# Attention maxima by pairs of 64-row matmuls into double banks, one accumulator bank, weighted values in threes, first pair head by head

## The chip, the cores and the metric

The kernel is one program on one core of a Trainium2 chip. Its metric is device time in microseconds (us) of one execution, from a single launch. PE is the matmul engine (PEld its weight loads), DVE the vector engine, ACT the scalar engine, POOL the general engine, SP the engine that issues most DMAs. PE writes its results to PSUM, which has eight banks of 512 fp32 columns on 128 partitions; DVE and ACT read them from there.

## What is computed

Attention over 8 batches of 8 heads, where two neighbouring queries are averaged first, and then a mixture of 8 experts on its output, each expert taking at most 576 tokens in the order of the gate's logits. Only the attention part is touched.

```python
q_pool = q.reshape(B, H, S // factor, factor, D).mean(axis=3)      # 8, 8, 576, 64
scores = scale * np.matmul(q_pool, k.transpose(0, 1, 3, 2))        # 576 x 1152 a head
scores = scores - np.max(scores, axis=-1, keepdims=True)
attn = np.exp(scores)
attn = attn / (np.sum(attn, axis=-1, keepdims=True) + 1e-09)
return np.matmul(attn, v).astype(np.float32)
...
logits = x @ w_gate
...
h = np.maximum(x[mask] @ w1[e], 0.0)
out[mask] = h @ w2[e]
```

## The kernel before

The 64 heads go in 32 pairs; the two heads of a pair lie one below the other on 128 partitions (64 dimensions each). A pair n has these stages.

- **Load and split** (`load`, `split`): queries `QD` and keys `KD` come in by DMA; DVE sums the query halves to `QS`; ACT rounds them to fp32r, `QH` and `KH`; the remainders become `QL` and `KL`. `spread` copies these by DMA into `KA`, `KB`, `QA`, `QB`, one head per slot, high and low parts stacked on 128 partitions.
- **Maxima** (`max_chunk`, line 401): for each block j of 64 queries of both heads a block-diagonal weight `BD[:, j]` (128 x 128) is multiplied with 384 keys of `KH`: 9 blocks times 3 chunks, 27 matmuls of 128 rows. They rotate through the PSUM banks `ma`, `mb`, `mc`, and DVE reduces each to a column of `MX` (line 405). For the first pair five more banks are used, and a third of the maxima goes to `MS` by ACT and is folded there (lines 408, 415, 417).
- **Shift** (`max_end`, `aug`): DVE takes the last maximum into `CM`, PE transposes it (line 437), DVE writes the shift `AU`, and two DMAs put it into row 64 of `QB`. The first pair does it without the DMA, with nine rows and the mask `ndiag` (line 432).
- **Scores** (`step`): 18 steps a pair, head s and key block kb of 128 keys. In each step, two halves of 288 queries: one matmul with `KA`, `QA` (line 466, 128 rows) and one with `KB`, `QB` (line 467, 65 rows) into one of three banks `sc`; ACT takes the exponential to `P` (line 470); POOL, for some steps DVE, computes the remainder `PM` (line 473).
- **Weighted values** (line 483): for every step, 5 query blocks times 3 f16 matmuls of 65 or 64 columns, accumulated over the head's 9 steps in the bank `av[s]`. They are issued for two steps at a time: 30 matmuls in a row. When a head is done, `evac` reads the bank on DVE (lines 506, 507, 510).
- **Gate** (every second pair): PE transposes the result (line 524), ACT copies it, three matmuls with 8 columns each go into strips of `av[1]` (line 536), DVE adds them to `LS`.

The order of the instructions on each engine is made by a planner, `Order`, from costs, priorities (`LEAD`) and due times (`LATE`) when the program is built; every engine then works through its own list in that order. Pair n+1's loads, splits and maxima are spread between pair n's steps. The experts (from line 670) follow with their own planner.

Of the kernel before, what the change touches and what calls it, by code (L numbers as in the profile page):

```python
# [46 lines left out]
class Order:  # L47
# [25 lines left out]
    def emit(self):  # L73
# [85 lines left out]
      0.5093}  # L159
LEAD = {"aug": 5.86, "augd": 4.23, "augt": -25.48, "av0a": 4.05, "bd": 8.85, "expa": -39.43, "expb": 17.79,  # L160
# [4 lines left out]
LATE = {"aug": 100, "augd": -300, "augt": 350, "av0a": 100, "bd": 1400, "expa": 50, "expb": -100, "fill": 3150,  # L165
# [69 lines left out]
def attention(ctx, tc, top, kt, qt, v, wg, x_dram, L, npair=NPAIR):  # L235
# [28 lines left out]
    BD = several(2, [128, NB, 128], FR, "BD")  # L264
# [21 lines left out]
    XT = several(3, [128, 3, 128], F32, "XT")  # L286
# [6 lines left out]
    ndiag = const.tile([128, NB, 64], F32, name="ndiag")  # L293
    iq = scratch[:, 1220:1220 + NB * 64].rearrange("p (a b) -> p a b", b=64)

    def fill(i, t):
        od.add(t, "POOL", 1000, lambda: nc.gpsimd.memset(BD[i].bitcast(F32), 0.0), w=[("BD", i, 0), ("BD", i, 1)], tag="fill")
        od.add(t + .1, "POOL", 100, lambda: nc.gpsimd.memset(CM[i], 0.0), w=[("CM", i, b) for b in range(3)], tag="fill")
        od.add(t + .2, "POOL", 1960, lambda: nc.gpsimd.memset(KB[i].bitcast(F32)[64:64 + NB], 1.0), w=[("KB1", i)], tag="fill")
        od.add(t + .3, "POOL", 90, lambda: nc.gpsimd.memset(V16[i][:, :, :, 128:129], 1.0),  # L300
               w=[("VH", i, 0), ("VH", i, 1)], tag="fill")
        if i == 0:
            od.add(t + .15, "POOL", 1060, lambda: nc.gpsimd.iota(iq, pattern=[[1, NB], [0, 64]], base=64, channel_multiplier=-1),
                   w=["iq"], tag="fill")
            od.add(t + .4, "DVE", 370, lambda: nc.vector.tensor_scalar(ndiag, iq, 0.0, -1.0, op0=OP.is_equal, op1=OP.mult),
                   r=["iq"], w=["ndiag"], tag="fill")
# [21 lines left out]
    def split(n, t):  # L328
# [41 lines left out]
    def values(n, t):  # L370
# [14 lines left out]
        od.add(t + AT["vs"] - 1, "DVE", 442, scale, r=["mb"], w=[("VS", i)], tag="vs")  # L385
# [9 lines left out]
    def max_chunk(n, j, c, z, t):  # L395
        i = n % 2
        banks = [(ma, "ma"), (mb, "mb"), (mc, "mc")]
        if n == 0:
            banks += [(sc[a], ("sc", a)) for a in range(3)] + [(av[b], f"av{b}") for b in range(2)]
        m, mk = banks[z % len(banks)]  # L400
        od.add(t, "PE", 175, lambda: nc.tensor.matmul(  # L401
            m[:, :384], BD[i][:, j, :], KH[i][:, 384 * c:384 * c + 384], start=True, stop=True),
            r=[("BD", i, 0), ("BD", i, 1)] + [("KH", i, z) for z in ((0,), (0, 1), (1,))[c]], w=[mk], tag="mm")
        if n or c < 2:
            od.add(t, "DVE", 464, lambda: nc.vector.tensor_reduce(MX[i][:, j, c:c + 1], m[:, :384], axis=AX.X, op=OP.max),  # L405
                   r=[mk], w=[("MX", i, j, c)], tag="mr")
        else:
            od.add(t, "ACT", 371, lambda: nc.scalar.copy(MS[:, j], m[:, :384]), r=[mk], w=[("MS", j)], tag="mc")

    def fold(j, t):  # L410

        m = MS[:, 3 * j:3 * j + 3]
        keys = [("MS", 3 * j + x) for x in range(3)]
        for z, w in enumerate((192, 96)):
            od.add(t + .01 * z, "DVE", 72 + .54 * w * 3, lambda w=w: nc.vector.tensor_tensor(
                m[:, :, :w], m[:, :, :w], m[:, :, w:2 * w], op=OP.max), r=keys, w=keys, tag="fold", lock=1)
        od.add(t + .05, "DVE", 70 + 300, lambda: nc.vector.tensor_reduce(
            MX[0][:, 3 * j:3 * j + 3, 2], m[:, :, :96], axis=AX.X, op=OP.max), r=keys, w=[("MX", 0, 3 * j + x, 2) for x in range(3)], tag="fold")

    def max_end(n, t):  # L420
        i = n % 2
        od.add(t, "DVE", 92, lambda: nc.vector.tensor_reduce(CM[i][:, 64:64 + NB], MX[i], axis=AX.X, op=OP.max),
               r=[("MX", i, j, c) for j in range(NB) for c in range(3)], w=[("CM", i, 2)], tag="fold")

    def aug(n, t):
        i = n % 2
        r = slice(64, 64 + NB)
        cm = [("CM", i, b) for b in range(3)]
        if n == 0:
            od.add(t, "PE", 110, lambda: nc.tensor.transpose(mb[:64 + NB, :128], CM[i][:, :64 + NB], ident), r=cm, w=["mb"], tag="augt")  # L430
            for s in range(2):
                od.add(t, "DVE", 670, lambda s=s: nc.vector.scalar_tensor_tensor(
                    QB[i][r, s].rearrange("p (a b) -> p a b", b=64),
                    mb[r, None, 64 * s:64 * s + 64].to_broadcast([NB, NB, 64]), -SHIFT, ndiag[r],
                    op0=OP.add, op1=OP.mult), r=["mb", "ndiag"], w=[("QB1", i, s)], tag="aug")
        else:
            od.add(t, "PE", 50, lambda: nc.tensor.transpose(mb[:NB, :128], CM[i][:, 64:64 + NB], ident), r=cm, w=["mb"], tag="augt")
            od.add(t, "DVE", 187, lambda: nc.vector.tensor_scalar(AU, mb[:NB, :128], -SHIFT, -1.0, op0=OP.add, op1=OP.mult),
                   r=["mb"], w=["AU"], tag="aug")
            for s in range(2):  # L440
                od.add(t, "SP", 830, lambda s=s: nc.sync.dma_start(
                    QB[i].bitcast(F32)[64:65, s].rearrange("p (a b) -> p a b", b=64), AU.bitcast(F32)[:, 64 * s:64 * s + 64]),
                    r=["AU"], w=[("QB1", i, s)], late=2000, tag="augd")
# [5 lines left out]
    def step(g):  # L449
# [10 lines left out]
        qr = [(x, i, s) for x in ("KA0", "KA1", "KB", "QA0", "QA1", "QB0", "QB1")] + [("KB1", i)]  # L460
# [15 lines left out]
        o, low, high = av[s], V16[i][:, s, kb, 0:D], V16[i][:, s, kb, D:2 * D + 1]  # L476
# [11 lines left out]
        behind.append((weighted, r, f"av{s}", kb == NKB - 1 and (n, s)))  # L488
        if g % 2:
            two = list(behind)  # L490
            behind.clear()
            od.cur = None
            od.add(g + LAG, "PE", 2 * 5 * 93, lambda: [x[0](range(5)) for x in two], r=two[0][1] + two[1][1],
                   w=[x[2] for x in two][:2 if s == 1 and kb == 0 else 1], tag="av0a", kind=1)
            for x in two:
                if x[3]:
                    evac(*x[3], g + LAG + 0.02)

    def evac(n, s, t):

        r, x = RS[s], X[n // 2 % NX][:, :, n % 2 * D:n % 2 * D + D]
        o = av[s][:, :325].rearrange("p (j d) -> p j d", d=65)
# [10 lines left out]
        od.add(t, "DVE", 346, recip, r=[f"av{s}", ("VS", n % 2)], w=[("RS", s)], tag="rc")  # L513
# [765 lines left out]
```

## Time and profile before

| | |
|---|---|
| median of 3 runs | 1342.98 us (1340.21 to 1343.5) |
| the profiled execution, its own time | 1342.09 us |
| its span, first to last instruction | 1340.3 us |
| PE busy | 97% of the span |
| DVE, ACT, POOL busy | 79%, 59%, 58% |
| attention with all 32 pairs under way | about 40 to 830 us of the span |

A row of a timeline has the start (us from the span's start), the duration, the engine, the line of the kernel, the operation, what it writes and reads, its shapes and how many like it follow each other. For a matmul 64\*128 means 64 rows of weights and 128 columns of them. Ends of matmuls are modelled: the next one starts long before, so their cost is read from one start to the next. In the grouped view, the two numbers behind the bar are busy us and mean ns of one.

### The profile page before, as it was taken

Reading aid. Unit: us, or ns where it says so; the run is one execution under the profiler, and the core shown is the slowest. Engines: PE = TensorE matmul, PEld = TensorE weight load, DVE = VectorE, ACT = ScalarE, POOL = GpSimd, SP = SyncE. Lnnn points to the kernel's source line nnn. Section 1 sums busy time; section 2 is a strip of 40 time slices with the busy share of each in tenths; the row PEclk is TensorE's granted clock in tenths of the full one; section 3 lists DMA queues with packets and bytes.
Section 4 is the critical chain, followed back from the end, with each engine's and each line's share of the span. In section 5 each row is a group of like instructions: output and inputs, shape, how many; then the busy total and the mean of one; then the engine's idle time right before and its main releaser. Section 6 shows DMA issues by size and latency. Waiting matters only on the chain.

```text
span 1340.3 us, 39670 instructions
## 1 busy us (share of the span) xinstructions
PE 1296.5 (97%) x15415; PEld 1169.3 (87%) x15415; DVE 1060.4 (79%) x2901; ACT 788.9 (59%) x1838; POOL 775.6 (58%) x739
## 2 busy tenths in 40 slices
PE   7999999999999999999999999699999999999996
PEld 6889999999999999999999898487979788798895
DVE  8999999999899999999999883788977767662220
ACT  4777777777777777777787765042343334244330
POOL 4555565665565665655655655064777676587631
PEclk8999999999999999999999999899999999999999
DMA  7877877877877877877877750044435343363400
GB/s 213 222 183 195 203 183 185 208 185 177 211 185 177 210 190 177 205 194 177 201 198 175 180 117 20 1 162 169 161 96 185 116 149 122 119 197 124 143 13 35
DMA packets 86841, 213.25 MB, mean 159 GB/s; under 512 B 12796, under 2 KB 37372, under 8 KB 84476
## 3 DMA queue, kind: packets, MB, share of 16 engines
q1 hardware_dynamic: 78172, 158.26, 47.9%
q0 software_dynamic: 8336, 52.44, 11.0%
q8 instruction: 121, 1.98, 0.6%
q14 instruction: 68, 0.56, 0.1%
q10 hardware_dynamic: 144, 0.02, 0.0%
HBM read 99.63 MB, written 18.87 MB: 88 GB/s over the span
## 4 chain that ended last, share of the span: by engine, by line
PE 86%; DVE 6%; DMA 3%; issue 2%; ACT 1%; POOL 0%; SPq 0%; POOLq 0%; DVEq 0%; ACTq 0%
PE av L483 18%; PE ph L1172 16%; PE po L1202 14%; PE sc L466 12%; PE sc L467 10%; PE mb L401 4%; PE mc L401 4%; PE ma L401 3%; DVE MX L405 2%; DMA KD<-in_kt_dram 2%; PE rt L845 1%; PE av L524 1%; PE po L1199 1%; PE av L536 1%; DMA KA<-KH 1%
## 5 line engine op out<-in xcount | busy, mean ns | idle before, releaser
L473 POOL TENSOR_TENSOR PM<-P 128x576 f16<-128x576 f32 x413 | 471.6, 1158 | 345.2 <-ACT P L470 328.1
L470 ACT ACTIVATE P<-sc 128x288 f32<-128x288 f32 x1152 | 433.9, 410 | 161.4 <-PE sc L467 128.1
L466 PE MATMUL sc<-QA,KA 128*128 128x288 f32 x1152 | 361.8, 321 | 2.3 <-ACT P L470 2.1
L467 PE MATMUL sc<-QB,KB 65*128 65x288 f32 (+1 forms) x1152 | 336.4, 298 | 3.1 <-issue 1.7
L483 PE MATMUL av<-V,P 128*128 128x65 f16 (+1 forms) x5760 | 304.0, 193 | 0.0
L483 PEld LDWEIGHTS <-P 128*128 128x128 bf16 x5760 | 270.3, 98 | 26.4 <-issue 2.2
L483 PE MATMUL av<-V,PM 128*128 128x65 f16 x2880 | 291.7, 194 | 0.5 <-DVE PM L473 0.5
L483 PEld LDWEIGHTS <-PM 128*128 128x128 f16 x2880 | 265.0, 97 | 0.6 <-DVE PM L473 0.6
L466 PEld LDWEIGHTS sc<-QA,KA 128*128 128x128 f32 x1152 | 220.4, 191 | 10.0 <-ACT P L470 6.7
L467 PEld LDWEIGHTS sc<-QB,KB 65*128 65x128 f32 (+1 forms) x1152 | 219.5, 191 | 3.9 <-issue 2.8
L1202 PE MATMUL po<-W2H,HX 128*128 128x512 f32 x512 | 167.4, 402 | 0.0
L405 DVE TENSOR_REDUCE MX<-ma 128x1 f32<-128x384 f32 x282 | 154.1, 547 | 14.6 <-PE ma L401 12.7
L405 DVE TENSOR_REDUCE MX<-mb 128x1 f32<-128x384 f32 x282 | 154.3, 547 | 10.0 <-PE mb L401 9.8
L405 DVE TENSOR_REDUCE MX<-mc 128x1 f32<-128x384 f32 x281 | 153.9, 548 | 3.1 <-PE mc L401 0.3
L1172 PE MATMUL ph<-XL,W1H 128*128 128x320 f32 (+1 forms) x512 | 152.5, 298 | 1.1 <-DVE XL L1071 1.1
L1172 PE MATMUL ph<-XH,W1H 128*128 128x320 f32 (+1 forms) x512 | 153.2, 299 | 0.0
L1172 PE MATMUL ph<-XH,W1L 128*128 128x320 f32 (+1 forms) x512 | 152.0, 297 | 0.0
L473 DVE TENSOR_TENSOR PM<-P 128x576 f16<-128x576 f32 x163 | 118.4, 748 | 12.4 <-ACT P L470 12.3
L1202 PE MATMUL po<-W2L,HX 128*128 128x512 f32 (+1 forms) x320 | 127.1, 397 | 0.0
L1177 ACT ACTIVATE HX<-ph 128x256 fp32r<-128x256 f32 (+1 forms) x128 | 52.2, 409 | 121.4 <-PE ph L1172 114.1
L1181 DVE SCALAR_TENSOR_TENSOR HX<-ph,HX 128x256 fp32r<-128x256 f32 x128 | 53.3, 419 | 75.9 <-ACT HX L1177 75.7
L1202 PEld LDWEIGHTS po<-W2H,HX 128*128 128x128 f32 x512 | 94.3, 189 | 17.1
(238 smaller groups left out, 2302.1 us busy)
## 6 DMA issues: line engine op xcount, KB each, us to landing
QD<-in_qt_dram SPq DMA_DIRECT2D x32, 576.0 KB
KD<-in_kt_dram SPq DMA_DIRECT2D x64, 288.0 KB
VD<-in_v_dram SPq DMA_DIRECT2D x32, 576.0 KB
KA<-KH SPq DMA_DIRECT2D x64, 288.0 KB
KB<-KH SPq DMA_DIRECT2D x64, 288.0 KB
KA<-KL SPq DMA_DIRECT2D x64, 288.0 KB
QA<-QH SPq DMA_DIRECT2D x128, 144.0 KB
QB<-QL SPq DMA_DIRECT2D x64, 144.0 KB
```

Source lines behind the costliest of these rows:

```text
L401: od.add(t, "PE", 175, lambda: nc.tensor.matmul(m[:, :384], BD[i][:, j, :], KH[i][:, 384 * c:384 * c + 384], start=True, stop=True), r=[(" ...
L405: od.add(t, "DVE", 464, lambda: nc.vector.tensor_reduce(MX[i][:, j, c:c + 1], m[:, :384], axis=AX.X, op=OP.max), r=[mk], w=[("MX", i, j, c ...
L466: nc.tensor.matmul(c[:, :288], KA[i][:, s, ks], QA[i][:, s, qs], start=True, stop=False)
L467: nc.tensor.matmul(c[:, :288], KB[i][:kr, s, ks], QB[i][:kr, s, qs], start=False, stop=True)
L470: od.add(g + 0.1 + 0.01 * t, "ACT", 293, lambda c=c, qs=qs: nc.scalar.activation(p[:, qs], c[:, :288], AF.Exp, scale=1.0 / 16), r=[ck], w= ...
L473: od.add(g + 0.2, en, dur, lock=1, fn=lambda: eng.tensor_tensor(pm, p, hi, op=OP.subtract), r=[("P32", g % NP, 0), ("P32", g % NP, 1)], w= ...
L483: nc.tensor.matmul(out, w[:, qs], v, start=kb == 0 and j == 0 and y == 0, stop=kb == NKB - 1 and y == 2, skip_group_check=True)
L524: nc.tensor.transpose(m[:, 128 * z:128 * z + 128], X[u][:, 3 * q + z], ident)
L1172: nc.tensor.matmul(p, a[:, d, fs], b[:, d, qs], start=z == 0, stop=z == 11)
L1177: nc.scalar.activation(HH[:, f, qs], p, AF.Relu)
L1181: V.scalar_tensor_tensor(HL[:, f, 64 + 256 * hf:320 + 256 * hf], p[:, :256], 0.0, h[:, :256], op0=OP.max, op1=OP.subtract)
L1202: nc.tensor.matmul(o[:n], a[:, z, q0:q0 + n], b[:, z], start=z == 0 and y == 0, stop=z == 7, skip_group_check=True)
```

## The change

1. The maxima of pairs 1 to 31 no longer use the block-diagonal weights for 8 of the 9 blocks. A block is now 128 queries of one head, taken from `QH` itself: 64 rows of weights, on partitions 0 to 63 for the first head and 64 to 127 for the second. One of each is issued next to the other, into the two banks of a double tile `mt[z]`. The queries 512 to 575 of both heads remain one 128-row block with `BD` (j = 4). So 27 matmuls of 128 rows become 24 of 64 rows and 3 of 128.
2. DVE reduces a double tile in one instruction: 13 of 768 columns and one of 384, in place of 27 of 384.
3. PSUM: three banks `sc`, one bank `av` for both heads in turn, two double tiles `mt`. The gate's transposes and matmuls use `mt` instead of `av`.
4. The weighted values are issued for three steps at a time (`"grp": [3, 6, 9]`), three blocks a head.
5. The first pair's maxima, folds and shift are done for head 0 and then for head 1.
6. `BD` shrinks from 9 blocks to one, so its copies by ACT do too; the shift is put into `QB` by three DMAs.
7. The planner's tables `LEAD` and `LATE` are new.

```diff
-    BD = several(2, [128, NB, 128], FR, "BD")
+    BD = several(2, [128, 128], FR, "BD")
...
-    av = [psum.tile([128, 512], F32, name=f"av{i}") for i in range(2)]
-    ma = psum.tile([128, 512], F32, name="ma")
-    mb = psum.tile([128, 512], F32, name="mb")
-    mc = psum.tile([128, 512], F32, name="mc")
+    av = psum.tile([128, 512], F32, name="av")
+    mt = [psum.tile([128, 2, 512], F32, name=f"mt{i}") for i in range(2)]
...
+    def product(n, j, c, out):
+        i = n % 2
+        ks = slice(384 * c, 384 * c + 384)
+        if j == 4:
+            nc.tensor.matmul(out, BD[i], KH[i][:, ks], start=True, stop=True)
         else:
+            s, b = j // 5, j % 5
+            h = slice(64 * s, 64 * s + 64)
+            nc.tensor.matmul(out, QH[i][h, 128 * b:128 * b + 128], KH[i][h, ks], start=True, stop=True)
...
+    def maxima(n, what, z, t, dur):
+        i = n % 2
+        m, mk = mt[z], f"m{z}"
+        def mm():
+            for y, (j, c) in enumerate(what):
+                product(n, j, c, m[:, y, :384])
+        od.add(t, "PE", dur, mm, r=needs(n, what), w=[mk], tag="mm")
...
+            src, dst, d = m[:, :, :384], MX[i][:, j:j + 6:5, c], 864
+        od.add(t, "DVE", d, lambda: nc.vector.tensor_reduce(dst, src, axis=AX.X, op=OP.max),
+               r=[mk], w=[("MX", i, j, c) for j, c in what], tag="mr")
...
-        if g % 2:
-            two = list(behind)
+        if kb + 1 in AT["grp"]:
+            some = list(behind)
...
-        for z in range(3 * NB):
-            max_chunk(n, z // 3, z % 3, z, at["mm"] + z * at["cw"])
+        if n:
+            for z in range(12):
+                maxima(n, [(z // 3, z % 3), (5 + z // 3, z % 3)], z % 2, at["mm"] + 2 * z * at["cw"], 230)
+            maxima(n, [(4, 0), (4, 1)], 0, at["mm"] + 24 * at["cw"], 350)
+            maxima(n, [(4, 2)], 1, at["mm"] + 26 * at["cw"], 175)
```

Three places of the order show how this falls out. On **PE**, in the middle of the attention, between two blocks of weighted values: `sc` rows are scores, `ma` and `mb` single maxima banks, `mt` a double tile. Before:

```order
L466 MATMUL sc_144<-QA_88,KA_84 128x288
L467 MATMUL sc_144<-QB_90,KB_86 128x288
L401 MATMUL ma<-KH_78,BD_92 128x384
L466 MATMUL sc_143<-QA_88,KA_84 128x288
L467 MATMUL sc_143<-QB_90,KB_86 128x288
```

and after, at a like place:

```order
L510 MATMUL sc_142<-QA_89,KA_85 128x288
L511 MATMUL sc_142<-QB_91,KB_87 128x288
L402 MATMUL mt_145<-KH_78,QH_81 128x384 x2
L510 MATMUL sc_141<-QA_89,KA_85 128x288
L511 MATMUL sc_141<-QB_91,KB_87 128x288
```

One 128-row matmul between scores has become two 64-row matmuls between scores. From the first weighted value on, the 64-row matmuls stand in 321 places of PE's list: 273 with one pair, 48 with two pairs behind each other. 212 of the 273 stand between scores as here, 42 between scores and a block of weighted values. Of the places where fp32r work follows a block of weighted values, 255 before (201 scores, 54 maxima) become 126 (89 scores, 1 full and 36 64-row maxima).

On **DVE**, the end of one pair's maxima, ahead of the last maximum into `CM`. Before:

```order
L405 TENSOR_REDUCE MX_116<-ma 128x1
L405 TENSOR_REDUCE MX_116<-mb 128x1
L405 TENSOR_REDUCE MX_116<-mc 128x1
L405 TENSOR_REDUCE MX_116<-ma 128x1
L542 TENSOR_TENSOR LS<-av_147,LS 72x384
```

and after:

```order
L429 TENSOR_REDUCE MX_115<-mt_146 128x2
L429 TENSOR_REDUCE MX_115<-mt_145 128x2
L388 SCALAR_TENSOR_TENSOR V_94<-VD_107,VS_103,V_94 128x9x64
L517 TENSOR_TENSOR PM_133<-P_123 128x576
L429 TENSOR_REDUCE MX_115<-mt_145 128x2
```

Each reduction now writes two maxima from two banks. On **SP**, the start of the list. Before, the second pair's queries (the second `QD` row) come behind the twelve copies of the first pair:

```order
L318 DMA QD_106<-in_qt_dram 128x1152
L321 DMA KD_105<-in_kt_dram 128x576 x2
L325 DMA VD_107<-in_v_dram 128x1152
L357 DMA KA_84<-KH_78 64x1152
L357 DMA KB_86<-KH_78 64x1152
```

and after, they stand ahead of them:

```order
L320 DMA QD_106<-in_qt_dram 128x1152
L323 DMA KD_105<-in_kt_dram 128x576 x2
L327 DMA VD_107<-in_v_dram 128x1152
L320 DMA QD_106<-in_qt_dram 128x1152
L355 DMA KA_84<-KH_78 64x1152
```

More of the change, by code (lines that the diff above doesn't have):

```diff
@@ L302, in fill, with places @@
         if i == 0:
[L303 to L306, printed above, removed]
+            for s in range(2):
+                def places(s=s):
+                    nc.gpsimd.iota(iq[:, s, :512].rearrange("p (a b) -> p a b", b=128), pattern=[[1, 4], [0, 128]],
+                                   base=64 + 5 * s, channel_multiplier=-1)
+                    nc.gpsimd.iota(iq[:, s, 512:], pattern=[[0, 64]], base=68, channel_multiplier=-1)
+                od.add(t + .15, "POOL", 1100, places, w=[("iq", s)], tag="iq")
+                od.add(t + .4, "DVE", 370, lambda s=s: nc.vector.tensor_scalar(
+                    ndiag[:, s], iq[:, s], 0.0, -1.0, op0=OP.is_equal, op1=OP.mult), r=[("iq", s)], w=[("ndiag", s)], tag="iq")
     def pads(t):
@@ L414, in fold, with maximum_out @@
+    def maximum_out(j, z, t):
+        m, mk = [(sc[0], ("sc", 0)), (sc[1], ("sc", 1)), (sc[2], ("sc", 2)), (av, "av")][z % 4]
+        od.add(t, "PE", 175, lambda: product(0, j, 2, m[:, :384]), r=needs(0, [(j, 2)]), w=[mk], tag="mm")
+        od.add(t, "ACT", 371, lambda: nc.scalar.copy(MS[:, j], m[:, :384]), r=[mk], w=[("MS", j)], tag="mc")
+    def fold(s, t):
+        a, g = (5, 4) if s else (0, 5)
+        m = MS[:, a:a + g]
+        keys = [("MS", a + x) for x in range(g)]
         for z, w in enumerate((192, 96)):
-            od.add(t + .01 * z, "DVE", 72 + .54 * w * 3, lambda w=w: nc.vector.tensor_tensor(
+            od.add(t + .01 * z, "DVE", 72 + .54 * w * g, lambda w=w: nc.vector.tensor_tensor(
@@ L421, in max_end @@
+    def max_end(n, t, s=None):
         i = n % 2
-        od.add(t, "DVE", 92, lambda: nc.vector.tensor_reduce(CM[i][:, 64:64 + NB], MX[i], axis=AX.X, op=OP.max),
-               r=[("MX", i, j, c) for j in range(NB) for c in range(3)], w=[("CM", i, 2)], tag="fold")
+        js = slice(0, NB) if s is None else slice(5, NB) if s else slice(0, 5)
+        od.add(t, "DVE", 92, lambda: nc.vector.tensor_reduce(CM[i][:, 64 + js.start:64 + js.stop], MX[i][:, js], axis=AX.X, op=OP.max),
+               r=[("MX", i, j, c) for j in range(js.start, js.stop) for c in range(3)], w=[("CM", i, 2 + (s or 0))], tag="fold")
@@ L425, in aug @@
     def aug(n, t):
         i = n % 2
[L427 to L443, printed above, removed]
@@ new lines, in aug, with head @@
+        cm = [("CM", i, 0), ("CM", i, 1), ("CM", i, 2)]
+        od.add(t, "PE", 50, lambda: nc.tensor.transpose(mt[1][:NB, 0, :128], CM[i][:, 64:64 + NB], ident), r=cm, w=["m1"], tag="augt")
+        od.add(t, "DVE", 187, lambda: nc.vector.tensor_scalar(AU, mt[1][:NB, 0, :128], -SHIFT, -1.0, op0=OP.add, op1=OP.mult),
+               r=["m1"], w=["AU"], tag="aug")
+        def head(s):
+            return lambda: nc.sync.dma_start(QB[i].bitcast(F32)[64:65, s, :512].rearrange("o (b x) -> o b x", x=128),
+                                             AU.bitcast(F32)[5 * s:5 * s + 4])
@@ L446, in attention, with tails @@
+        def tails():
+            nc.sync.dma_start(QB[i].bitcast(F32)[64:65, :, 512:], AU.bitcast(F32)[4:5].rearrange("o (s x) -> o s x", x=64))
+        for s in range(2):
+            od.add(t, "SP", 700, head(s), r=["AU"], w=[("QB1", i, s)], late=2000, tag="augd")
+        od.add(t, "SP", 700, tails, r=["AU"], w=[("QB1", i, 2)], late=2000, tag="augd")
     LAG = AT["lag"]
@@ L486, in step @@
         r = [("P32", g % NP, 0), ("P32", g % NP, 1), ("PM", g % NM), ("VH", i, s), ("VL", i, s)]
-        behind.append((weighted, r, f"av{s}", kb == NKB - 1 and (n, s)))
-        if g % 2:
-            two = list(behind)
+        behind.append((weighted, r))
+        if kb + 1 in AT["grp"]:
+            some = list(behind)
             behind.clear()
             od.cur = None
[L493 to L497, printed above, removed]
+            od.add(g + LAG, "PE", 461 * len(some), lambda: [x[0](range(5)) for x in some], r=[y for x in some for y in x[1]],
+                   w=["av"], tag="av0a", kind=1)
+            if kb == NKB - 1:
+                evac(n, s, g + LAG + 0.02)
     def evac(n, s, t):
         r, x = RS[s], X[n // 2 % NX][:, :, n % 2 * D:n % 2 * D + D]
-        o = av[s][:, :325].rearrange("p (j d) -> p j d", d=65)
+        o = av[:, :325].rearrange("p (j d) -> p j d", d=65)
         xk = [("X", n // 2 % NX, n % 2, s), ("X4", n // 2 % NX, n % 2)]
@@ L530, in gate @@
-    def gate(n, t):
+            for x, q in enumerate(qs):
+                for y in range(3):
+                    nc.tensor.transpose(m[:, x, 128 * y:128 * y + 128], X[u][:, 3 * q + y], ident)
+        od.add(t, "PE", 250 * k, tr, r=xk, w=[f"m{z}"], tag="gt")
+        od.add(t, "ACT", 362 if k == 1 else 680, lambda: nc.scalar.copy(XT[:, qs[0]:qs[0] + k], m[:, :k, :384]),
+               r=[f"m{z}"], w=[("XT", q) for q in qs], tag="gc")
+    def gate(n, t, z):
         bp, c = n // H, n % H // 2
+        m = mt[z][:, 0]
@@ L548, in gate_back @@
         bp = n // H
+        m = mt[z][:, 0]
         def back():
-            for z in range(3):
-                nc.tensor.transpose(m[:, 96 * z:96 * z + 64 + E], LS[:, 128 * z:128 * z + 128], ident[:64 + E, :64 + E])
+            for y in range(3):
+                nc.tensor.transpose(m[:, 96 * y:96 * y + 64 + E], LS[:, 128 * y:128 * y + 128], ident[:64 + E, :64 + E])
         def put():
@@ L556, in put, with gate_last @@
                                   m[:, :288].rearrange("p (z q e) -> p z q e", z=3, e=32)[:, :, :, :E])
-        od.add(t, "PE", 220, back, r=["LS"], w=[mk], tag="gb")
-        od.add(t, "DVE", 140, put, r=[mk], w=[("L", bp, q) for q in range(3)], tag="gp")
-    def gate_last(n, q, t):
+        od.add(t, "PE", 155, back, r=["LS"], w=[f"m{z}"], tag="gb")
+        od.add(t, "DVE", 140, put, r=[f"m{z}"], w=[("L", bp, q) for q in range(3)], tag="gp")
+    def gate_last(n, q, t, z):
         bp, c = n // H, n % H // 2
-        m, mk = ((mb, "mb"), (ma, "ma"), (mb, "mb"))[q]
+        m = mt[z][:, 0]
         def mm():
-            for z in range(3):
-                nc.tensor.matmul(m[:, E * z:E * z + E], XT[q][:, z], wgs[:, c], start=z == 0, stop=z == 2,
+            for y in range(3):
+                nc.tensor.matmul(m[:, E * y:E * y + E], XT[:, q, 128 * y:128 * y + 128], wgs[:, c], start=y == 0, stop=y == 2,
                                  skip_group_check=True)
```

156 lines of the change are left out of this document (81 added, 75 removed), and 10 rows, old and new, of tables (LATE, LEAD).

## The prediction

> **What bounds the kernel now.** I read the page first, then a table of busy times by stage, then the chain of waits of the middle stage.
>
> ```profile
> PE 1296.5 (97%) x15415; PEld 1169.3 (87%) x15415; DVE 1060.4 (79%) x2901; ACT 788.9 (59%) x1838; POOL 775.6 (58%) x739
> 68.00:400.00 332.00, 328.27 (x4968) 307.66 (x4967) 312.59 (x695) 255.45 (x611) 195.18 (x180) 1.00 0.77 191
> 400.00:760.00 360.00, 359.12 (x5442) 336.69 (x5442) 335.06 (x730) 279.85 (x671) 211.73 (x187) 1.00 0.78 191
> ```
>
> The lower rows are two stretches of the attention: length, busy time of PE, PEld, DVE, ACT and POOL, granted clock, DMA share, GB/s. Between 400 and 760 us PE idles 0.9 us of 360, at full clock. DVE comes next with 93%, DMA has 0.78. So in the attention PE's own issue time sets the pace, and what the change does there is a sum over PE's list. The experts are not touched. How PE spends its time is seen in the timeline of PE:
>
> ```profile
> 499.82 0.34 PE L401 MATMUL ma<-KH,BD 128*128 128x384 f32 x1
> 500.00 0.29 PE L466 MATMUL sc<-QA,KA 128*128 128x288 f32 x1
> 500.13 0.30 PE L467 MATMUL sc<-QB,KB 65*128 65x288 f32 x1
> 500.36 0.82 PE L536 MATMUL av<-XT,wgs 128*8 128x384 f32 x6
> 501.12 0.44 PE L401 MATMUL mb<-KH,BD 128*128 128x384 f32 x1
> 501.40 0.34 PE L401 MATMUL mc<-KH,BD 128*128 128x384 f32 x1
> 501.57 0.30 PE L466 MATMUL sc<-QA,KA 128*128 128x288 f32 x1
> 503.28 0.19 PE L483 MATMUL av<-V,PM 128*128 128x65 f16 x1
> 503.31 0.38 PE L466 MATMUL sc<-QA,KA 128*128 128x288 f32 x1
> 503.53 0.29 PE L467 MATMUL sc<-QB,KB 65*128 65x288 f32 x1
> ```
>
> From start to start, a maxima matmul takes 0.178 us (499.82 to 500.00, 501.40 to 501.57) and a scores matmul 0.13. The first scores matmul behind a block of weighted values takes 0.22 (503.31 to 503.53), 0.085 more: its weights could not be loaded early enough.
>
> **The change on PE.** The question is what two 64-row matmuls cost that stand alone between matmuls of 128 rows. None of the old maxima is of that kind, but the trace has two neighbours. One is the gate (L536 above), whose three matmuls use three strips of 8 columns of the array, in two rounds; the other is the transposes of a 64-row tail in the experts, four in a row between full matmuls:
>
> ```profile
> 882.67 0.28 PE L1172 MATMUL ph<-XH,W1L 128*128 128x256 f32 x1
> 882.78 0.28 PE L1172 MATMUL ph<-XH,W1H 128*128 128x256 f32 x1
> 882.99 0.46 PE L1062 MATMUL ph<-ident,XG 64*128 64x64 f32 x4
> 883.38 0.39 PE L1172 MATMUL ph<-XL,W1H 128*128 128x256 f32 x1
> 883.60 0.28 PE L1172 MATMUL ph<-XH,W1L 128*128 128x256 f32 x1
> L1062 PE MATMUL ph<-ident,XG 64*128 64x64 f32 x8 | 0.9, 235 | 0.0
> L536 PE MATMUL av<-XT,wgs 128*8 128x384 f32 x90 | 12.4, 488 | 0.0
> ```
>
> An L1172 here has a slot of 0.12 (882.67 to 882.78). The 64-row group begins 0.21 after the last one: 0.09 late. One record is 0.235 long and four cover 0.46, so the fourth starts 0.225 after the first, at 883.215, with a slot of 0.075. It is through at 883.29, and the next full matmul starts at 883.38: again 0.09 late. That matmul then takes 0.22 to the next instead of 0.12: its weights weren't loaded ahead. The gate shows the same three prices: in, 500.36 instead of 500.26; out, the second round starts 0.82 - 0.49 = 0.33 behind the first and lasts 0.33, so it is through at 501.02, and L401 starts at 501.12; then 0.28 instead of 0.18. So every visit to a part of the array costs **0.09 to get in, 0.09 to get out, and 0.10 for the first weights afterwards**. A pair pays 0.10 for its own first weights too (128 fp32r columns, as with L401 at 501.12). Narrow operands alone don't do it:
>
> ```profile
> 943.33 0.39 PE L1202 MATMUL po<-W2L,HX 128*64 128x512 f32 x1
> 943.56 0.39 PE L1199 MATMUL po<-W2H,HX 128*128 128x512 f32 x1
> ```
>
> The 64-column matmul is followed 0.23 later, with no stall; in the built program its instruction names the whole array, while those of L1062 and of the new maxima name 64 rows of it.
>
> The Trainium skill, page "TensorEngine Tiling (Array Packing)", section "Key Properties", says that a change of tiling mode, not just of the tile, drains TensorE. By that rule an isolated pair pays a drain on both sides; the trace agrees, with 0.09 us each way.
>
> Inside a visit the two halves can run together: the gate's six matmuls, of 384 columns each like L401, all start within 0.33, where six in turn would need at least 5 x 0.178 = 0.89 from the first start to the last. So strips do run side by side. I take 0.185 for the pair, one slot and a little. An isolated pair then costs 0.09 + 0.10 + 0.185 + 0.09 + 0.10 = **0.565 us, against 2 x 0.178 = 0.356** for the two full matmuls it replaces: +0.21. Bounds from the nearest rows: below, no stall and no late weights, 0.185 (-0.17); above, the second half's weights wait another 0.10 and the halves run in turn, 0.84 (+0.48). Into a block of weighted values the way back is cheaper:
>
> ```profile
> L483 PEld LDWEIGHTS <-P 128*128 128x128 bf16 x5760 | 270.3, 98 | 26.4 <-issue 2.2
> L466 PEld LDWEIGHTS sc<-QA,KA 128*128 128x128 f32 x1152 | 220.4, 191 | 10.0 <-ACT P L470 6.7
> ```
>
> The f16 weight load is 0.09 shorter, so I take 0.07 off there. The sum over the places counted in PE's list:
>
> - 231 single pairs that return to fp32 work: 231 x 0.21 = +48.5 us;
> - 42 that return to weighted values: 42 x 0.14 = +5.9;
> - 48 visits of two pairs, nearly all before weighted values: 0.38 + 2 x 0.185 - 0.07 = 0.68 against 4 x 0.178 = 0.71: -1.5;
> - late weights behind weighted values, 255 places before and 90 after (the 36 places with pairs carry theirs already): -165 x 0.085 = -14.0.
>
> Together +39 us. The three remaining full maxima, the scores and the weighted values themselves are as many as before.
>
> **The other parts.** Their cover is PE's full list.
>
> ```profile
> L405 DVE TENSOR_REDUCE MX<-mb 128x1 f32<-128x384 f32 x282 | 154.3, 547 | 10.0 <-PE mb L401 9.8
> L510 DVE TENSOR_TENSOR X<-av,RS 128x320 f32<-128x320 f32 x32 | 15.4, 480 | 0.0
> L510 DVE TENSOR_TENSOR X<-av,RS 128x256 f32<-128x256 f32 x32 | 13.3, 414 | 0.1
> 406.73 0.20 DVE L506 TENSOR_SCALAR RS<-av,VS 128x5 f32<-128x5 f32 x1
> 407.51 0.48 DVE L510 TENSOR_TENSOR X<-av,RS 128x320 f32<-128x320 f32 x1
> ```
>
> DVE: 64 more columns cost 66 ns (the two L510 rows), so 384 more cost 0.40 and a double reduction 0.95. A pair needs 13 x 0.95 + 0.55 = 12.9 us instead of 27 x 0.547 = 14.8. DVE has less to do in a longer time: nothing on the path. If PE became faster instead, DVE would be at 95%.
>
> The one accumulator bank adds a wait: the next head's first weighted values wait for L506 to L510, 1.26 us (406.73 to 407.99), and behind them in PE's list waits everything. At each of the 63 changes of head, PE's list has scores, maxima and gate work of 2.2 us or more between the two blocks (at the slots above), mostly 3.5 to 5. That covers it; without cover it would cost up to 1.3 us a head, 80 us in all. With two double tiles a pair may wait for DVE's 0.95 us; successive pairs stand apart by scores or weighted values of a like length, so I cost it at nothing. The smaller `BD` copies free ACT, and the third DMA a pair adds an issue on SP; neither is waited for by PE in the stretch above.
>
> The start can gain:
>
> ```profile
> 24.54 0.76 DVE L330 TENSOR_TENSOR QS<-QD 128x576 f32<-128x576 f32 x1 [2.99 <-DMA QD<-in_qt_dram]
> 25.77 0.37 PE L466 MATMUL sc<-QA,KA 128*128 128x288 f32 x1
> ```
>
> DVE stands 2.99 us before the second pair's queries, ahead of the first pair's last maximum in its list, and the first scores begin at 25.77. Now these queries are fetched earlier and head 0 goes first. I take -4 us, between 0 (the second pair's loads and splits set the pace instead) and -8.
>
> **Sum**: 1342.09 (the profiled execution, 0.9 below the median of 1342.98) + 39 - 4 = 1377; against the median, **1378 us**.
>
> **The rivals.**
>
> *The halves overlap and nothing stalls.* The Trainium skill, page "TensorE: Matmul & The Clock Gate", section "Measured speedup vs the span model", gives tiles in different row groups one matmul's duration plus about 4 ns for each further tile, and says nothing of a cost for entering. As a mechanism of this kernel: 369 pairs at 0.185 for 0.356 give -63 us, -14 and -4 as above, 1262; with DVE at 95% some of it is lost to waits for the two double tiles, and I put it at 1270. For it: the gate's strips do overlap. Against it: both visits to a part of the array in this trace stall. It decides for faster as soon as a visit's overhead is below 0.17. Chance 0.19.
>
> *The halves' weights load one after the other.* 321 visits x 0.10 more: 1410. For it, two loads with nothing in their way, 0.11 apart in full mode:
>
> ```profile
> 501.11 0.19 PEld L401 LDWEIGHTS mb<-KH,BD 128*128 128x128 f32 x1 [0.65 <-DVE MX L405]
> 501.22 0.19 PEld L401 LDWEIGHTS mc<-KH,BD 128*128 128x128 f32 x1
> ```
>
> Against it: no row shows two wide loads in different halves. Chance 0.27.
>
> *The halves do not overlap at all.* Then 369 x 0.17 more on top of the forecast: 1440. Chance 0.05.
>
> *The pairs neither stall nor overlap*, so the change does nothing for the maxima: -14 - 4, 1325. Chance 0.04.
>
> **How the numbers follow.** My forecast has 0.45. The range reaches from 1330 to 1442: it holds the three stalling cases and leaves out the two faster ones and some error of size. About 0.3% is what a measurement of this kernel can tell from no change. Faster by more: 0.19 and the last rival's 0.04, less a little, 0.21. Within 0.3%: 0.03. Slower: 0.76.
>
> **What would show it.** In PE's timeline after, the 64-row rows start 0.2 us or more behind a scores matmul, and the scores behind them take 0.23 to the next instead of 0.13; the two 64-row rows start within 0.01 of each other if their weights load together, 0.11 apart if not. Between 400 and 760, PE stays over 98% busy and DVE falls below 90%. If the rows show scores directly behind a pair at 0.13, the stall is wrong and the time will be near 1270. If PE idles before the first weighted values of a head, the single bank costs what I left out.

## The result and the profile after

The changed kernel takes **1412.47 us** (median of 4 runs, 1400.1 to 1415.71) beside 1343.17 us for the kernel before (1340.21 to 1343.5): a ratio of 1.0504, 95% interval 1.0439 to 1.0569. It is 69 us slower, where +35 was forecast. The profiled execution took 1412.39 us, its span is 1410.6 us.

First the page's busy times and the table by stage, for the kernel after (columns as in the prediction: length, busy time of PE, PEld, DVE, ACT and POOL, granted clock, DMA share, GB/s):

```profile
PE 1367.6 (97%) x15416; PEld 1129.5 (80%) x15416; DVE 1048.8 (74%) x2488; ACT 750.0 (53%) x1825; POOL 777.1 (55%) x742
50.00:145.00 95.00, 88.13 (x1061) 70.42 (x1061) 73.32 (x135) 51.96 (x129) 41.55 (x45) 0.84 0.63 158
400.00:760.00 360.00, 359.00 (x5036) 291.63 (x5032) 305.11 (x501) 243.06 (x617) 200.31 (x176) 1.00 0.73 178
```

and the early stretch in the kernel before:

```profile
50.00:145.00 95.00, 90.06 (x1310) 82.67 (x1307) 90.65 (x211) 69.12 (x165) 55.52 (x57) 1.00 0.75 190
```

In the middle PE is as full as it was (359.00 of 360) and finishes fewer matmuls (5036 instead of 5442): the time is lost while PE is listed as busy. In the early stretch there is something else: the granted clock is 0.84 where it was 1.00.

Next the timeline of PE in the kernel after, in the middle of the attention:

```profile
508.04 0.38 PE L510 MATMUL sc<-QA,KA 128*128 128x288 f32 x1
508.26 0.29 PE L511 MATMUL sc<-QB,KB 65*128 65x288 f32 x1
508.48 0.44 PE L402 MATMUL mt<-KH,QH 64*128 64x384 f32 x2
508.85 0.40 PE L510 MATMUL sc<-QA,KA 128*128 128x288 f32 x1
509.09 0.30 PE L511 MATMUL sc<-QB,KB 65*128 65x288 f32 x1
509.23 0.30 PE L510 MATMUL sc<-QA,KA 128*128 128x288 f32 x1
```

The pair (L402, x2) starts 0.22 behind the scores matmul instead of 0.13: 0.09 to get in. The next scores matmul starts 0.37 after the pair, and takes 0.24 to its successor instead of 0.13 (509.09 to 509.23 is the plain slot): 0.10 for late weights. 0.09 + 0.37 + 0.10 is 0.56 us for the pair, and 0.565 was forecast. The x2 shows that both halves are one entry: their recorded starts lie 3 to 4 ns apart. So do the starts of their weight loads:

```profile
508.48 0.19 PEld L402 LDWEIGHTS mt<-KH,QH 64*128 64x128 f32 x2 [0.16 <-DVE MX L429]
```

At the end of the attention the kernel after is 71 us behind (the last head ends at 904.3 instead of 833.6). How they are spread is read from the end of each pair's second head, where DVE takes the sums. In the kernel before, the first pair, pair 4 and pair 31:

```profile
60.43 0.22 DVE L506 TENSOR_SCALAR RS<-av,VS 128x5 f32<-128x5 f32 x1 [1.21 <-PE av L483]
142.56 0.22 DVE L506 TENSOR_SCALAR RS<-av,VS 128x5 f32<-128x5 f32 x1
814.51 0.23 DVE L506 TENSOR_SCALAR RS<-av,VS 128x5 f32<-128x5 f32 x1 [4.63 <-PE av L483]
```

and the first pair, pair 4 and pair 31 in the kernel after:

```profile
56.57 0.22 DVE L549 TENSOR_SCALAR RS<-av,VS 128x5 f32<-128x5 f32 x1 [1.03 <-PE av L527]
158.26 0.21 DVE L549 TENSOR_SCALAR RS<-av,VS 128x5 f32<-128x5 f32 x1
883.20 0.23 DVE L549 TENSOR_SCALAR RS<-av,VS 128x5 f32<-128x5 f32 x1 [3.33 <-PE av L527]
```

From pair 4 to pair 31 a pair took (814.51 - 142.56) / 27 = 24.89 us and takes 26.85: **+1.96 us a pair, 53 us**. The first pair ends at 56.57 instead of 60.43: **-3.9 us**. Pairs 2 to 4 take 101.7 instead of 82.1 us: **+19.6 us**, in the stretch with the low clock. The last pair adds 2.

Two rows of the waits show the rest: first the weight loads of the kernel after,

```profile
PEld sc L510 <- ACT P L514: 47.1, 218, 1.1
PEld mt L402 <- DVE MX L429: 13.0, 45, 1.8
```

then those of the kernel before (us in all, times, longest):

```profile
PEld sc L466 <- ACT P L470: 6.7, 17, 1.1
```

Scores now wait 218 times for ACT to free a score bank, against 17. The view lists no wait of a weighted value (L527) for DVE's reading of the one bank `av`: at the 63 changes of head, the new head's first one starts 0.14 us or more after DVE's last read, 3.2 at the median.

### The profile page after: what moved, and what is told of

It is laid out like the page before. It is cut to its first block, busy times and chain, and to the rows that moved or that the text cites. A ratio compares the mean times of both kernels' runs of the same rounds, so it can differ in the third digit from the quotient of the medians.

```text
span 1410.6 us, 39129 instructions
## 1 busy us (share of the span) xinstructions
PE 1367.6 (97%) x15416; PEld 1129.5 (80%) x15416; DVE 1048.8 (74%) x2488; ACT 750.0 (53%) x1825; POOL 777.1 (55%) x742
## 3 DMA queue, kind: packets, MB, share of 16 engines
q1 hardware_dynamic: 77676, 158.26, 45.8%
## 4 chain that ended last, share of the span: by engine, by line
PE 87%; DVE 5%; issue 3%; DMA 1%; ACT 1%; POOL 1%; SPq 1%; DVEq 0%; POOLq 0%; ACTq 0%
PE av L527 18%; PE sc L510 16%; PE ph L1224 15%; PE po L1254 13%; PE sc L511 10%; PE mt L402 8%; DVE MX L429 2%; PE rt L897 1%; PE mt L398 1%; PE mt L569 1%; PE po L1251 1%; ACT P L514 1%; DVE PM L517 1%; PE mt L583 1%; SPq L355 1%
## 5 line engine op out<-in xcount | busy, mean ns | idle before, releaser
L514 ACT ACTIVATE P<-sc 128x288 f32<-128x288 f32 x1152 | 414.5, 411 | 261.4 <-PE sc L511 232.2
L429 DVE TENSOR_REDUCE MX<-mt 128x2 f32<-128x768 f32 (+1 forms) x443 | 402.2, 926 | 108.1 <-PE mt L402 88.6
L510 PE MATMUL sc<-QA,KA 128*128 128x288 f32 x1152 | 382.7, 346 | 3.1 <-ACT P L514 1.7
L511 PE MATMUL sc<-QB,KB 65*128 65x288 f32 (+1 forms) x1152 | 330.0, 299 | 0.0
L527 PE MATMUL av<-V,P 128*128 128x65 f16 (+1 forms) x5760 | 295.6, 194 | 0.0
L527 PEld LDWEIGHTS <-P 128*128 128x128 bf16 x5760 | 274.0, 99 | 25.4 <-issue 18.4
L527 PE MATMUL av<-V,PM 128*128 128x65 f16 x2880 | 286.3, 196 | 0.8
L527 PEld LDWEIGHTS <-PM 128*128 128x128 f16 x2880 | 267.6, 98 | 2.5 <-DVE PM L517 2.5
L402 PE MATMUL mt<-KH,QH 64*128 64x384 f32 x760 | 162.5, 436 | 6.1 <-DVE MX L429 4.1
L517 DVE TENSOR_TENSOR PM<-P 128x576 f16<-128x576 f32 x163 | 125.2, 785 | 11.5 <-ACT P L514 11.1
L402 PEld LDWEIGHTS mt<-KH,QH 64*128 64x128 f32 x760 | 71.0, 187 | 60.9 <-issue 36.6
```

Source lines behind the costliest of these rows:

```text
L402: nc.tensor.matmul(out, QH[i][h, 128 * b:128 * b + 128], KH[i][h, ks], start=True, stop=True)
L429: od.add(t, "DVE", d, lambda: nc.vector.tensor_reduce(dst, src, axis=AX.X, op=OP.max), r=[mk], w=[("MX", i, j, c) for j, c in what], tag="mr")
L510: nc.tensor.matmul(c[:, :288], KA[i][:, s, ks], QA[i][:, s, qs], start=True, stop=False)
L511: nc.tensor.matmul(c[:, :288], KB[i][:kr, s, ks], QB[i][:kr, s, qs], start=False, stop=True)
L514: od.add(g + 0.1 + 0.01 * t, "ACT", 293, lambda c=c, qs=qs: nc.scalar.activation(p[:, qs], c[:, :288], AF.Exp, scale=1.0 / 16), r=[ck], w= ...
L517: od.add(g + 0.2, en, dur, lock=1, fn=lambda: eng.tensor_tensor(pm, p, hi, op=OP.subtract), r=[("P32", g % NP, 0), ("P32", g % NP, 1)], w= ...
```

## The experiments

Theory: the 64-row visits cost what they were forecast to cost, and on top come scores and maxima that wait for banks, and the low clock. Rivals: the one accumulator bank, the double tiles or the threes are the cost; the price comes per pair and not per visit; the halves do not overlap. Where nothing else is said, an experiment keeps the order of the instructions on every engine. The kernel before was timed beside each group of experiments: 1342.54 us beside the first four, 1340.33 beside the next four (two pairs with the order held, all visits in the kernel before, short exponentials, short exponentials with all rows) and 1343.31 beside the last two. Small differences between groups are taken from these.

### All 128 rows

```diff
-            h = slice(64 * s, 64 * s + 64)
+            h = slice(0, 128) if n else slice(64 * s, 64 * s + 64)
```

> The kernel after, but in pairs 1 to 31 the 64-row maxima matmuls take all 128 rows of QH and KH, so that a maximum is that of the two heads' summed scores (the shift of the exponentials is then another one). The order on all engines is that of after. Visits theory (each isolated 64-row pair costs 0.56 us for 0.36): 231 x 0.21 + 42 x 0.14 - 1.5 = 53 us less, 1359 us; down to 1345 if the half clock of the first 140 us goes with the visits, up to 1375 if scores that wait for ACT take a part back. Rival (one accumulator bank, double tiles, threes or the table of priorities cost the time): stays at 1400 to 1415. In the trace the scores matmul in front of a maxima matmul should be followed 0.13 later again, not 0.22.

Measured: **1363.44 us** (1362.09 to 1365.06), ratio to the kernel before 1.0156 (1.0133 to 1.0178): 49 us less. Its timeline at a maximum between scores:

```profile
490.46 0.30 PE L511 MATMUL sc<-QB,KB 65*128 65x288 f32 x1
490.60 0.51 PE L402 MATMUL mt<-KH,QH 128*128 128x384 f32 x2
490.95 0.29 PE L510 MATMUL sc<-QA,KA 128*128 128x288 f32 x1
491.08 0.30 PE L511 MATMUL sc<-QB,KB 65*128 65x288 f32 x1
```

The stalls are gone: 0.14 in, 0.35 for two, 0.13 behind. From pair 4 to pair 31 a pair takes 25.46 us, 1.39 less than in the kernel after; pairs 2 to 4 take 87.8 instead of 101.7, and the granted clock from 50 to 145 us is 0.97 instead of 0.84. So the 64-row form costs 49 of the 69 us, part of them by way of the clock, and the bank, the tiles and the threes do not cost the bulk. 21 us are left.

### Both halves on the same rows

```diff
-            h = slice(64 * s, 64 * s + 64)
+            h = slice(64 * s if n == 0 else 0, 64 * s + 64 if n == 0 else 64)
```

> The kernel after, but in pairs 1 to 31 both 64-row matmuls of a pair use rows 0 to 63 (the first head's queries and keys), so that the second head's maxima are the first head's. Order as in after. If the two halves run side by side in after, they now run in turn: 372 pairs x about 0.17 = +63 us, 1475 us. If they ran in turn already (no overlap), 1412 us stays. The stalls at both ends of a visit should stay at 0.09 each.

Measured: **1472.37 us** (1466.4 to 1474.13), 60 more than after.

```profile
509.06 0.29 PE L511 MATMUL sc<-QB,KB 65*128 65x288 f32 x1
509.29 0.61 PE L402 MATMUL mt<-KH,QH 64*128 64x384 f32 x2
509.83 0.40 PE L510 MATMUL sc<-QA,KA 128*128 128x288 f32 x1
510.07 0.30 PE L511 MATMUL sc<-QB,KB 65*128 65x288 f32 x1
510.20 0.30 PE L510 MATMUL sc<-QA,KA 128*128 128x288 f32 x1
```

The visit lasts 0.54 (509.29 to 509.83) instead of 0.37; the 0.23 in front and the 0.24 behind stay. The halves of the changed kernel do run side by side. In turn, the parts of a visit can be read one by one: the second matmul starts 0.279 after the first, the next full one 0.265 after the second (medians of 273 visits). Beside a slot of 0.178 that is 0.10 for the visit's own first weights and 0.09 to get out, as forecast.

### Two pairs a visit, and weighted values in twos

Two pairs as one item of the planner:

```diff
-            for z in range(12):
-                maxima(n, [(z // 3, z % 3), (5 + z // 3, z % 3)], z % 2, at["mm"] + 2 * z * at["cw"], 230)
+            for z in range(0, 12, 2):
+                pair_of_pairs(n, z, at["mm"] + 2 * z * at["cw"])
```

> The kernel after, but two successive 64-row pairs are one item of PE's list, into both double tiles: 186 visits in place of 321, all with four 64-row matmuls. If the price is one per visit (0.38 us), 135 x 0.38 = 51 us less: 1361 us, up to 1385 if PE now waits for both reductions (1.9 us) of the visit before. Rival, the price is one per pair or per matmul (weights that load alone): 1412 us or more.

Twos:

```diff
-      0.5093, "grp": [3, 6, 9]}
+      0.5093, "grp": [2, 4, 6, 8, 9]}
```

> The kernel after, but the weighted values are issued for two steps at a time (2, 4, 6, 8, 9 of a head's nine) in place of three. Visits theory with scores that wait for ACT as a side cost: 128 more blocks with late weights are +11 us, shorter bursts of scores (four halves in place of six) give 10 to 18 back: 1400 to 1415 us. Rival, the threes are the main cost: below 1385 us.

Measured: **1595.34 us** (1590.03 to 1597.62) and **1580.82 us** (1575.68 to 1583.86). Both expectations missed by far. These two edits let the planner make a new order. The middle stretch, first with two pairs as one item, then with twos:

```profile
400.00:760.00 360.00, 323.09 (x3996) 264.82 (x3997) 250.17 (x396) 195.48 (x487) 164.88 (x139) 0.84 0.58 140
```

```profile
400.00:760.00 360.00, 337.29 (x4295) 273.63 (x4294) 266.33 (x415) 204.96 (x520) 171.98 (x146) 0.90 0.59 147
```

PE idles 37 and 23 us of 360 and has clocks of 0.84 and 0.90; in the kernels before and after it idled 1. The order is another one on every engine, and it is full of waits; `LEAD` and `LATE` were made for the items of the kernel after. Neither run says anything on visits or threes. What follows is only that such a part has to be tried with the order held.

### Two pairs a visit, order held

The order is made as in the kernel after. Then, as it is issued, the first 64-row pair of each two is held back to the second, with its reduction:

```diff
-        for i in order:
-            items[i][4]()
+        held = []
+        for i in order:
+            x, k = items[i], self.mark.get(id(items[i][4]))
+            if k and k[1] == "mm" and not held:
+                held.append(x)
+            elif k and k[1] == "mm" and self.mark[id(held[0][4])][0] == k[0]:
+                held.insert(1, x)
+                flush()
+            elif k and k[1] == "mr" and held and x[5][0] == held[0][6][0]:
+                held.append(x)
...
```

> The kernel after with its order as made, then only the maxima moved: the first 64-row pair of each two is held back to the place of the second, with its reduction behind both, unless a data dependence forbids it. 200 visits in place of 322, all else in the same order. If the price is per visit (0.38 us), 122 x 0.38 = 46 us less: 1366 us, up to 1385 if reductions now come late for the shift or the next visit. Rival, the price is per pair: 1412 us; if held reductions set the pace, above.

Measured: **1449.05 us** (1448.44 to 1454.07), 37 more than after (39 beside the kernel before of its own group). Its middle stretch, then its weight loads' waits (mt L424 is the 64-row pair, mt L594 the gate's transposes):

```profile
400.00:760.00 360.00, 341.02 (x4782) 278.62 (x4780) 284.10 (x480) 227.56 (x584) 191.36 (x165) 0.98 0.68 168
```

```profile
PEld sc L535 <- ACT P L539: 64.0, 214, 1.1
PEld mt L594 <- DVE MX L451: 20.3, 15, 1.9
PEld mt L424 <- DVE MX L451: 19.0, 62, 1.6
```

At full clock a visit of two pairs takes 0.55 from its first start to the next matmul (median), against two times 0.37 and a second set of stalls: the price is per visit, in the slots. But PE idles 19 us of 360. Of these, 12.7 stand where a held pair had to be issued by itself right in front of another user of the double tiles, a gate transpose (L594) or the one-column matmul of `values` (L396), which then waits about 1.05 us for its reduction. Half clock covers 58 us of the attention, 44 in the kernel after. So this move of the maxima alone gains nothing; another might.

### A visit by itself, in the kernel before

Every maximum of pairs 1 to 31 on half the rows:

```diff
-            m[:, :384], BD[i][:, j, :], KH[i][:, 384 * c:384 * c + 384], start=True, stop=True),
+            m[:, :384], BD[i][:64, j, :], KH[i][:64, 384 * c:384 * c + 384], start=True, stop=True) if n else nc.tensor.matmul(m[:, :384], BD[i][:, j, :], KH[i][:, 384 * c:384 * c + 384], start=True, stop=True),
```

> The kernel before, and in pairs 1 to 31 every maxima matmul takes only rows 0 to 63 of its weights and keys: 837 matmuls of 64 rows, in 702 visits of PE's list (575 of one, 121 of two, the rest longer), order as before; the second head's maxima are then not its own (products with the zero blocks of BD). Nothing else of the change is in it, so it prices a visit alone. Theory A, a visit pays 0.09 in, 0.09 out and 0.10 for the weights behind it, and the 0.10 inside a pair is the second half's weights: 702 x 0.28, about 12 off where weighted values follow or precede, 135 x 0.10 more inside the longer visits: +198, 1540 us, and a single 64-row matmul is followed 0.265 later. Theory B, the 0.10 inside is the visit's own first weights: 702 x 0.38 - 12 + 135 x 0.10 = +268, 1610 us, and it is followed 0.37 later. Rival, the price comes with the pair or with another part of the change: below 1360 us.

Measured: **1735.37 us** (1729.42 to 1742.6), above both theories, and the scores behind a single 64-row matmul start 0.369 later (median): theory B in the slots. The time has a second part. Three neighbouring stretches of 3.4 us in that kernel:

```profile
487.80:491.20 3.40, 3.40 (x35) 2.17 (x34) 3.17 (x6) 2.26 (x6) 1.67 (x2) 1.00 0.92 192
491.20:494.60 3.40, 3.40 (x26) 2.12 (x21) 1.74 (x4) 1.28 (x4) 1.65 (x2) 1.00 0.97 257
494.60:498.00 3.40, 3.40 (x35) 2.76 (x35) 1.35 (x4) 0.82 (x2) 1.80 (x2) 0.51 0.39 100
```

PE has no idle time, and the clock falls to half all the same. Half clock covers 372 us of the attention here, 10 in the kernel before.

The same with 5 of 27 maxima:

```diff
-            m[:, :384], BD[i][:, j, :], KH[i][:, 384 * c:384 * c + 384], start=True, stop=True),
+            m[:, :384], BD[i][:64, j, :], KH[i][:64, 384 * c:384 * c + 384], start=True, stop=True) if n and c == 1 and j % 2 == 0 else nc.tensor.matmul(m[:, :384], BD[i][:, j, :], KH[i][:, 384 * c:384 * c + 384], start=True, stop=True),
```

> The kernel before, and in pairs 1 to 31 only 5 of the 27 maxima matmuls (chunk 1 of the blocks 0, 2, 4, 6, 8) take 64 rows: 155 visits, all of a single matmul; order as before; for those columns the second head's maxima are not its own. With so few visits the granted clock should stay as before, so the time gives the price without it: 155 x 0.38 less 2 where weighted values stand beside = +57, 1398 us. Rival, the 135 us by which every maximum with 64 rows came out above its sum (1735 for about 1600) are the price of the visits themselves, and not the half clock seen there: 155 / 702 x 395 = +87, 1428 us.

Measured: **1389.06 us** (1387.86 to 1389.95), ratio 1.0343 (1.0321 to 1.0365): +45.8 us for 155 visits, 0.295 each, below both values. From 35 us to the end of the attention it has full clock, as the kernel before has. A visit between scores:

```profile
505.77 0.29 PE L467 MATMUL sc<-QB,KB 65*128 65x288 f32 x1
506.00 0.44 PE L401 MATMUL mb<-KH,BD 64*128 64x384 f32 x1
506.36 0.40 PE L466 MATMUL sc<-QA,KA 128*128 128x288 f32 x1
506.60 0.30 PE L467 MATMUL sc<-QB,KB 65*128 65x288 f32 x1
506.74 0.34 PE L402 MATMUL mc<-KH,BD 128*128 128x384 f32 x1
```

0.23 + 0.36 + 0.24 = 0.83, less 0.135 + 0.178 + 0.133 for the three slots without a stall, is 0.38 as expected, but only half of the visits stand so. Behind a gate's strips nothing is paid to get in, in front of weighted values little for late weights. Weighted over the places the slots give 0.35. The last 0.05 may be time in which PE would have waited elsewhere; that isn't shown. With 0.30 a visit, the 702 visits above come to 211 of 395 us; half clock over 362 us more than before is worth up to 181. Together they would make 392: the sum fits, though the two were not tried apart in that kernel. One thing more: a single 64-row matmul is followed after 0.36 to 0.37, a pair in two halves after 0.37. **The second half is free; everything paid is the visit.**

### Shorter exponentials, shorter reductions

Exponentials:

```diff
-                p[:, qs], c[:, :288], AF.Exp, scale=1.0 / 16), r=[ck], w=[("P32", g % NP, t)], tag="exp" + "ab"[t])
+                p[:, qs.start:qs.start + (144 if n else 288)], c[:, :144 if n else 288], AF.Exp, scale=1.0 / 16), r=[ck], w=[("P32", g % NP, t)], tag="exp" + "ab"[t])
```

> The kernel after, but from the second pair on each exponential is taken over 144 of its 288 columns (the other columns of P keep old values), so ACT frees the score banks sooner. Order as in after. If scores that wait for ACT cost 0.6 us a pair, 15 to 20 us less in the steady stretch, and the half clock of the first 140 us may go as well: 1380 to 1397 us. Rival, those waits are made up for elsewhere: 1405 to 1415 us.

Measured: **1398.34 us** (1397.84 to 1401.66), 14 less than after (11 beside the kernel before of its own group), just above what was expected. A pair takes 26.52 us instead of 26.85, which is half of what was hoped for, and 24 us of half clock stay between 40 us and the end of the attention, 31 in the kernel after. The row of ACT's exponentials among the waits of the weight loads falls:

```profile
PEld sc L510 <- ACT P L514: 26.0, 120, 1.0
```

Together with all 128 rows:

> Both edits: all 128 rows in the maxima of pairs 1 to 31 (summed scores of both heads) and the exponentials over 144 of 288 columns. If the 64-row visits and the scores that wait for ACT are all that the change costs, 1363 less 15 to 25: 1338 to 1348 us, about the time before. Rival, something else of the change (the one accumulator bank, the double tiles, the threes) holds the rest: it stays at 1355 to 1365 us.

Measured: **1351.64 us** (1350.15 to 1353.47), ratio 1.0089 (1.0072 to 1.0106): between the two expectations. Of the 21 us that all 128 rows had left, 11 stay beside the 1340.33 us of this group (9 beside 1342.54, as the next expectation counts them). So DVE's double reductions were shortened too:

```diff
-            src, dst, d = m[:, :, :384], MX[i][:, j:j + 6:5, c], 864
+            src, dst, d = m[:, :, :192 if n else 384], MX[i][:, j:j + 6:5, c], 864
```

> All 128 rows in the maxima of pairs 1 to 31 (summed scores), exponentials over 144 of 288 columns, and the double reductions over 192 of each 384 columns, so that DVE frees the two double tiles sooner. Order as in after. If maxima that wait for the double tiles hold the last 9 us above the time before, 1340 to 1346 us; rival, the rest lies in the early pairs and the issue of the weighted values in threes: 1348 to 1354 us.

Measured: **1343.16 us** (1340.16 to 1344.76), ratio 1.0002 (0.9991 to 1.0012): the time before. Maxima that wait for the two double tiles, and what waits for DVE behind them, hold the rest. Part of it is in the early pairs, as the rival had it: pairs 2 to 4 take 82.2 us instead of 88.4, and each later pair 24.97 instead of 25.18. In this kernel bursts of scores still wait now and then:

```profile
316.07 0.29 PE L510 MATMUL sc<-QA,KA 128*128 128x288 f32 x1
316.21 0.29 PE L511 MATMUL sc<-QB,KB 65*128 65x288 f32 x1
316.41 0.40 PE L510 MATMUL sc<-QA,KA 128*128 128x288 f32 x1
316.64 0.30 PE L511 MATMUL sc<-QB,KB 65*128 65x288 f32 x1
```

This is the fourth half of a burst, and there are three score banks. It starts 0.06 late, and its second matmul is 0.10 late on top (316.41 to 316.64 instead of 0.13), as behind a block of weighted values.

No version that was run is faster than the kernel before.

## Why the prediction was right, and where it was short

**The mechanism and the sign were right.** The isolated pair measured 0.56 us, part by part as forecast: 0.09 in, 0.37, 0.10 behind, and the same-rows run splits the 0.37 into own weights, slot and way out. The rivals fall: there is a stall (against the 1270), the halves' weights start to load 4 ns apart, not 0.11 (against the 1410), and the halves overlap (against the 1440). The time alone would have misled: 1412 lies on the 1410 of a rival whose mechanism the rows refute. That is chance. PE stays full and DVE is at 85% in the middle. The Trainium skill, page "TensorEngine Tiling (Array Packing)", section "Key Properties", has a drain at a change of mode: the trace agrees, 0.09 each way. The section "Theoretical Speedup" of the same page of the Trainium skill gives up to 2 times for dimensions of at most 64. Here the two halves do overlap, and the isolated pair still takes 0.56 where two full matmuls take 0.356: the measurement decides, and it is a loss.

**The size was short, 35 for 69**, and the range held because it was wide. Per pair of heads in the steady stretch the forecast was +39 / 31 = 1.26 us and the measurement +1.96. By its terms:

- *Visits*: +52.9 us forecast (48.5 + 5.9 - 1.5), 1.71 a pair; all 128 rows gave back 1.39. Somewhat too large; perhaps a stall covers part of waits that come anyway.
- *Late weights behind the weighted values*, -14.0 us or -0.45 a pair: **this step failed**. There are fewer such places, but the threes leave six score halves in a row for three banks. With visits, long exponentials and long reductions all taken away, a pair still took 24.97, not less than 24.89. Counted by neighbours over 16 pairs of that kernel and of the kernel before, 4.0 places a pair fewer with late weights save 0.34, and the slots of scores and maxima that follow one another are 0.39 longer in all. The gain was counted without its other side. The threes weren't tried alone with the order held, so what they cost by themselves stays open.
- *ACT*, "neither is waited for by PE": true in the stretch that was read, not after the change. Short exponentials took 0.28 a pair off (0.33 off the kernel after).
- *DVE and the double tiles*, taken as nothing: the double reduction lasts 0.96 at the median, 0.95 was forecast, but its cover does not hold everywhere. Short reductions took off 0.21 a pair.

1.39 + 0.28 + 0.21, and 0.08 that remain, are the 1.96.

**The early pairs were left out.** The start came as forecast (-3.9 us for -4; the first scores at 22.28 instead of 25.77, and DVE sums the second pair's queries at 15.37 without a wait). But pairs 2 to 4 lose 19.6 us, and a granted clock of 0.84 over 95 us is worth 15 of them. The forecast had no term for the clock, which was 1.00 in that stretch before. All 128 rows take 13.9 of the 19.6 back, and short reductions 6.2 more. Waits such as these in the kernel after stand shortly ahead of a fall at 126 us; that they cause it is not shown:

```profile
118.89 0.62 PE L402 MATMUL mt<-KH,QH 64*128 64x384 f32 x4 [1.04 <-DVE AU L476]
124.09 0.44 PE L402 MATMUL mt<-KH,QH 64*128 64x384 f32 x2 [1.69 <-DVE MX L429]
```

The four runs of the changed kernel had mean clocks of 0.978, 0.975, 0.988 and 0.978 and took 1412.4, 1415.7, 1400.1 and 1412.5 us: their spread goes with the clock.

**The one accumulator bank** cost nothing, as forecast.

## What to carry to other kernels

In these kernels half-height matmuls pay per visit, not per matmul: 0.38 us between full matmuls, against 0.18 saved for each pair. Two pairs a visit take 0.09 + 0.55 + 0.10 = 0.74 us for 0.71 and just fail to pay; by these numbers a group that pays must be longer, and needs as many free banks. When items are gathered into longer blocks, count the other blocks that become longer with them, and the buffers those turn over. A planner's table belongs to its items: try a part of a change with the order held, or the new order is what gets measured.

## What was not expected of the hardware

The clock fell to half while PE had no idle time by the profile. To see what goes before a fall, the twelve kernels (the two and the ten experiments) were cut into stretches of 3.413 us, the step in which the recorded clock changes. Those at full clock between 40 and 800 us (to 1200 us in the kernel with all maxima on 64 rows) were sorted by whether half clock came next. For each, the columns that its matmuls stream were divided by 2.16 a ns (288 in 0.133 us), weighted with their rows out of 128, and taken as a share of the stretch.

Of the 70 stretches ahead of a fall, 69 have a share of at most 0.42 (16 in the kernel with all maxima on 64 rows, 0.35 to 0.42). Of the 2445 that stayed at full clock, 10 lie below 0.42. A single limit, at 0.41, sorts all but 9 of them; without the weight by rows the best limit leaves 32 on the wrong side. So rows seem to count for the clock, and a stall inside a visit seems to count as nothing done. This is a sorting of what happened, not a trial of that cause alone.

The Trainium skill, page "TensorE: Matmul & The Clock Gate", section "Part 1: The HAM clock gate", has a gate that goes by how busy PE was in windows of 3413 ns; the steps here fit such windows (in the kernel after, half clock lasts 3.41, 6.83, 10.24 or 13.65 us at a time). The same page of the Trainium skill, section "Why this matters for your kernels", advises no idle gaps of about 3 us between bursts of matmuls. That would not have been enough here: in the stretch ahead of the fall shown above PE was listed as busy 3.40 us of 3.40.
